# Normalizing the query features ahead of their transpose, in a fused linear-attention and MLP kernel

## The chip, the core and the metric

The kernel runs on one core of a Trainium2 chip. The metric is the device time of one execution in microseconds (us). PE is TensorE's matrix array (PEld its weight load), DVE is VectorE, ACT is ScalarE, POOL is GpSimd, SP is SyncE, which here only issues DMAs. PSUM is the memory that PE writes to, in eight banks.

## The reference, cut to what matters

```
x: 1 x 2048 x 448, bf16; H = 16 heads, Dh = 28
xn = layernorm(x)
q, k, v = split(xn @ wqkv)                       # per head 28 columns
phi(t) = [softmax(t @ w_phi), softmax(-t @ w_phi)]     # 2 x 28 features of a head
kv = phi(k)^T v ;  z = sum over tokens of phi(k)
o  = (phi(q) kv) / (phi(q) z + 1e-6)
out = x + o @ wo + mish(xn @ w1 + b1) @ w2       # w1: 448 x 1792, w2: 1792 x 448
```

## The kernel before, in words

The 2048 tokens make 16 tiles of 128 (t = 0 to 15), worked on in pairs (u = 0 to 7). All of x, the weights and the hidden activations `actT` (14 chunks x 2048 tokens) stay in SBUF. The work is cut into some 340 named steps, and a written-out list, `ORDER`, gives the order in which they are issued. Every engine then works through its own part of that order, strictly in sequence, and waits on semaphores where a step needs another's result. Nothing is scheduled at run time, so a step that waits holds everything behind it on its engine. DMAs of one queue are issued in the same manner: nearly all by SP.

The steps, by their names in `ORDER`:

- `lx..`, `lkm`, `lvm`, `lkt`, `lqT`, `l1..`, `l2`, `lo`: loads. The last letter is the queue (s for SP, a for ACT). `lqT0` to `lqT3` load the q weights transposed.
- `st`, `rs`, `xn`, `xt`: statistics of a pair (DVE, some tiles on ACT), reciprocal root (ACT or POOL), normalizing (DVE or POOL), and the transpose of the normalized pair (PE and an evacuation, or a DMA).
- `wtk`, `wmk`, `wmq`, `qd`, `bd`: w_phi is multiplied into the k and q weights once, giving `Wpk` and `Wpq`. This setup uses PE transposes (L556), passes L580 and evacuations L510/L512; `qd` (L286) doubles the last columns of the transposed q weights ahead of the q part.
- `k`, `v`, `q` with the parts A, B and H: projections of a pair. Each pass uses 64 rows of the array, two run at once (L423). The evacuation of k and q is the exponential on ACT, once with scale 1 and once with -1 (L618, L680).
- `kn`: one half (sign) of a pair's key exponentials is summed per head (DVE, L626), inverted (L628) and multiplied (POOL, L630).
- `kv`: phi(k)^T v of a pair, 32 small passes on 32-column strips of the array (L649). `kvz` copies the sum over all pairs out (L660) and turns it by a DMA into `KVZ` (L666).
- `e`: a DMA turns a tile's query exponentials (L688). There are three buffers for a pair's exponentials: `Eq0` and two rows of `actT`.
- `nd`: numerators and denominators of a query tile. 16 passes of 60 columns (L722) make, for each head and each sign, the numerator, the denominator and, by a column of ones, the sum of the query exponentials. Because two heads share a pass, half of `KVZ` is zero blocks. DVE then copies the sums, crosses them with the other sign's numerators, adds, inverts and scales (L738 to L749).
- `ot`, `wo`: the transpose of the output of a pair and its product with wo (L845, 64 rows).
- `f`: the MLP's first product, 64-row passes of 512 columns, with Mish and bias on ACT as evacuation (L699). `g`: its second product, 14 passes on all 128 rows into the same banks as `wo` (L828).
- `sto`, `stt`: stores, behind the last addition (L793).

## Time and profile before

| | us |
|---|---|
| median of 3 runs | 151.07 (150.71 to 151.2) |
| span of the profiled execution | 148.7 |
| PE busy | 144.0 |
| DVE busy | 102.7 |
| ACT busy | 74.7 |
| POOL busy | 38.9 |

The span runs from the first to the last instruction. The profiled execution's own device time is not recorded apart from its span; the median of the runs stands beside it, 2.4 us above. An engine's busy time is no measure of what it costs: what counts is which engine the chain of waits passes through. In the profile a line number is that of the kernel file, PS is PSUM, "SPq" is the issuing of a DMA by SP, and a transposed or plain load is done only when it has landed.

### The profile page before, as it was taken

The numbers are of one execution on the slowest core, as the hardware profiler recorded it, in microseconds if no ns is written. First come the engines' busy times: TensorE is split into PE (matmuls) and PEld (weight loads), VectorE is DVE, ScalarE is ACT, GpSimd is POOL, SyncE is SP. The second block draws the span as 40 slices with busy tenths as digits, with TensorE's granted clock in tenths as the row PEclk, the third lists the DMA queues.
The fourth block names the chain that finished last, engine by engine and source line by source line (L and its number), as shares of the span: only waits on it lengthen the run. The fifth ranks groups of instructions, "written<-read, shape, count | busy, mean of one in ns | idle before, by whom it ended". The sixth has DMA issues, their size and how long they took to land.

```text
span 148.7 us, 3864 instructions
## 1 busy us (share of the span) xinstructions
PE 144.0 (97%) x1669; PEld 74.2 (50%) x1669; DVE 102.7 (69%) x229; ACT 74.7 (50%) x91; POOL 38.9 (26%) x53
## 2 busy tenths in 40 slices
PE   6899999999999999999999999999999999999992
PEld 2365555555444555444444445545555555555561
DVE  0699898996999930407787989529983999930072
ACT  4997999779999999567747661002000000000000
POOL 4424465179999992000000000000000000000000
PEclk9999999999999999999999999999999999999999
DMA  4997997799699069499956053210013130551005
GB/s 131 245 278 216 119 185 149 126 170 344 103 188 196 14 52 132 85 239 295 195 98 125 4 62 62 43 23 0 7 37 86 35 93 0 123 127 58 4 10 175
DMA packets 39964, 17.23 MB, mean 116 GB/s; under 512 B 33932, under 2 KB 39180, under 8 KB 39948
## 3 DMA queue, kind: packets, MB, share of 16 engines
q1 hardware_dynamic: 39776, 16.89, 54.4%
q8 instruction: 13, 0.21, 0.6%
q10 hardware_dynamic: 172, 0.10, 0.2%
q14 instruction: 3, 0.02, 0.0%
HBM read 7.02 MB, written 1.84 MB: 60 GB/s over the span
## 4 chain that ended last, share of the span: by engine, by line
PE 92%; DMA 3%; DVE 2%; SPq 1%; issue 0%
PE PS L423 50%; PE PS L828 29%; PE PS L845 7%; DMA Wkv<-in_A_wqkv_dram 3%; PE PS L722 3%; PE PS L649 2%; PE PS L580 1%; DVE xn L497 1%; SPq L270 1%; PE PS L556 0%; PE PS L505 0%; DVE x_all L793 0%; DVE Eq L512 0%; DVE x_all L814 0%
## 5 line engine op out<-in xcount | busy, mean ns | idle before, releaser
L423 PE MATMUL PS<-xnT,W 64*128 64x512 bf16 x392 | 44.8, 377 | 0.0
L828 PE MATMUL PS<-W,actT 128*128 128x448 bf16 (+1 forms) x224 | 42.9, 351 | 0.0
L699 ACT ACTIVATE actT<-PS,b1T 128x1024 bf16<-128x1024 f32 x28 | 29.8, 1112 | 22.1 <-PE PS L423 22.1
L828 PEld LDWEIGHTS PS<-W,actT 128*128 128x128 bf16 x224 | 21.5, 98 | 19.8 <-issue 0.3
L423 PEld LDWEIGHTS PS<-xnT,W 64*128 64x128 bf16 x392 | 17.9, 94 | 21.9 <-PE PS L423 1.9
L630 POOL TENSOR_TENSOR actT<-actT,rSk 128x896 bf16<-128x896 bf16 x16 | 26.6, 1699 | 5.1 <-DVE rSk L628 5.1
L793 DVE TENSOR_TENSOR x_all<-PS,x_all 128x448 bf16<-128x448 f32 (+1 forms) x16 | 9.2, 613 | 15.2 <-PE PS L845 10.5
L626 DVE TENSOR_REDUCE Sk<-actT 128x32 f32<-128x896 bf16 x16 | 16.6, 1037 | 1.1 <-ACT actT L618 1.1
L618 ACT ACTIVATE actT<-PS 128x896 bf16<-128x896 f32 x16 | 13.7, 920 | 1.8 <-PE PS L423 1.7
L423 PE MATMUL PS<-Wpk,xnT 64*128 64x448 bf16 x112 | 13.2, 349 | 0.0
L423 PE MATMUL PS<-Wkv,xnT 64*128 64x448 bf16 x112 | 12.9, 349 | 0.0
L423 PE MATMUL PS<-Wpq,xnT 64*128 64x448 bf16 x112 | 12.6, 349 | 0.0
L738 DVE COPY Sq<-PS 128x16 f32<-128x16 f32 x32 | 4.0, 167 | 12.0 <-PE PS L722 12.0
L462 DVE BATCH_NORM_STATS2 stats<-x_all 128x6 f32<-128x448 bf16 x14 | 8.4, 601 | 3.4 <-DMA x_all<-in_A_x_dram 3.4
L746 DVE TENSOR_TENSOR v_all<-v_all 128x464 f32<-128x464 f32 x16 | 10.3, 641 | 0.6
L742 DVE TENSOR_TENSOR v_all<-PS,Sq 128x464 f32<-128x464 f32 x16 | 10.3, 641 | 0.5
L749 DVE TENSOR_TENSOR xn<-v_all,rden 128x448 bf16<-128x448 f32 x16 | 10.0, 625 | 0.6
L744 DVE TENSOR_TENSOR v_all<-PS,Sq 128x464 f32<-128x464 f32 x16 | 10.1, 629 | 0.0
L680 ACT ACTIVATE actT<-PS 128x896 bf16<-128x896 f32 x10 | 8.6, 930 | 0.1
L423 PEld LDWEIGHTS PS<-Wpq,xnT 64*128 64x128 bf16 x112 | 5.4, 94 | 5.0 <-ACT actT L680 0.2
L423 PEld LDWEIGHTS PS<-Wkv,xnT 64*128 64x128 bf16 x112 | 5.4, 94 | 5.1 <-ACT actT L618 0.2
L423 PEld LDWEIGHTS PS<-Wpk,xnT 64*128 64x128 bf16 x112 | 5.3, 94 | 5.1 <-issue 0.2
(83 smaller groups left out, 118.8 us busy)
## 6 DMA issues: line engine op xcount, KB each, us to landing
W<-in_B_w_dram SPq DMA_DIRECT2D x1, 1568.0 KB, 7.9
out_dram<-x_all SPq DMA_DIRECT2D x7, 224.0 KB, 2.2
W<-in_B_w_dram SPq DMA_DIRECT2D x1, 1344.0 KB, 7.0
x_all<-in_A_x_dram SPq DMA_DIRECT2D x4, 224.0 KB, 3.1
x_all<-in_A_x_dram SPq DMA_DIRECT2D x2, 448.0 KB, 4.9
Wkv<-in_A_wqkv_dram SPq DMA_DIRECT2D x2, 336.0 KB, 4.8
Wo<-in_A_wo_dram SPq DMA_DIRECT2D x2, 336.0 KB, 6.3
W<-in_B_w_dram SPq DMA_DIRECT2D x2, 224.0 KB, 4.1
```

The source lines that it names most:

```text
L423: ins = e.matmul(o, lhs(c, k), rhs(c, k), start=first and n == at[par][0], stop=last and n == at[par][-1])
L618: op("ACT", lambda e, s=s: e.activation(E_of(u)[:, s, :, :], two(b, D), ACT.Exp, scale=1.0 if s == 0 else -1.0), r=[pb(b), pb(b + 1)], w=[ ...
L626: op("DVE", lambda e: e.tensor_reduce(Sk[u][:, s, :], Eh(), AX.X, ALU.add), r=[("E", u, s)], w=[("Sk", u, s)], tag=f"Sk{u}.{s}")
L630: op("POOL", lambda e: e.tensor_tensor(Eh(), Eh(), ap_on(rSk[u][:, s, 0:1], [[1, 2 * H], [0, DH]]), ALU.mult), r=[("E", u, s), ("rSk", u, ...
L699: op("ACT", lambda e: e.activation(actT[:, fc, q * 1024:(q + 1) * 1024], bank(b, 2), ACT.Mish, bias=b1T[:, fc:fc + 1]), r=[("b1T",), pb(b) ...
L742: op("DVE", lambda e: e.tensor_tensor(tv(t1[i]), num(0), sx(1), ALU.mult), r=[pb(b), pb(b + 1), ("Sq", i, 1)], w=[("t1", i)], tag=f"ta{t}")
L744: op("DVE", lambda e: e.tensor_tensor(tv(t2), num(1), sx(0), ALU.mult), r=[pb(b), pb(b + 1), ("Sq", i, 0)], w=[("t2",)], tag=f"tb{t}")
L746: op("DVE", lambda e: e.tensor_tensor(t1[i], t1[i], t2, ALU.add), r=[("t1", i), ("t2",)], w=[("t1", i)], tag=f"tc{t}")
L749: op("DVE", lambda e: e.tensor_tensor(o_sb[(t // 2) % 2][:, t % 2, :].rearrange("p (h d) -> p h d", d=DH), t1[i][:, :, 0:DH], ap_on(rden[i ...
L793: op("DVE", lambda e: e.tensor_tensor(x_all[:, t, 0:n], bank(b)[:, 0:n], x_all[:, t, 0:n], ALU.add), r=[pb(b), ("x", t)], w=[("out", t)], ...
L828: ins = e.matmul(bank(b)[:, 0:width(t)], actT[:, fc, tok(t)], W2[:, fc, 0:width(t)], start=first and fc == 0, stop=last and fc == FC - 1)
L845: ins = e.matmul(bank(b)[:, 0:w], oT_of(u)[lo:hi, cc * P:(cc + 1) * P], Wo[lo:hi, cc, 0:w], start=first and n == at[par][0], stop=last and ...
```

## The change

- The query exponentials of a tile are now normalized ahead of the transpose (new step `qn`, one for each tile: sum and reciprocal on DVE, product on POOL, as for the keys). Both signs of a head lie side by side in 56 of 64 columns, so that a pass takes one head's whole feature row.
- `nd` keeps its 16 passes for a tile, but each has 30 columns. On DVE a reciprocal and one product are left. `KVT` and `KVZ` are half as large and have no zero blocks.
- `nd`'s results go to four buffers in place of two.
- `ORDER` is new throughout. Loads are the same, but x tiles 4 to 7 are issued by ACT and the others stand in another order; the statistics, normalizings and evacuations are dealt out otherwise (all v evacuations on ACT); `g` and `kv` are grouped otherwise.
- Options for other loads (`lkv`, `lfr`) and for a reciprocal root by single tiles are added, but no step of the list uses them; the bank choice is moved into a class with the same rules.

The core of the diff:

```
-NDW = 2 * (DH + 2)
+NDC = DH + 2
...
+    def q_norm(u, i):
+        n = u % 3
+
+        def Ei():
+            return Eq_of(u)[:, i, :, 0:QP].rearrange("p h (s f) -> p h s f", s=2)
+        op("DVE", lambda e: e.tensor_reduce(Sq[u][:, i, :].rearrange("p (h s) -> p h s", s=2), Ei(), AX.X, ALU.add),
+           r=[("Eq", n, i, s) for s in range(2)], w=[("Sq", u, i)], tag=f"Sq{u}.{i}")
+        op("DVE", lambda e: e.reciprocal(Sq[u][:, i, :], Sq[u][:, i, :]), r=[("Sq", u, i)], w=[("rSq", u, i)],
+           tag=f"rSq{u}.{i}")
+        op("POOL", lambda e: e.tensor_tensor(Ei(), Ei(), ap_on(Sq[u][:, i, 0:1], [[2, H], [1, 2], [0, DH]]), ALU.mult),
+           r=[("Eq", n, i, s) for s in range(2)] + [("rSq", u, i)], w=[("Eq", n, i, s) for s in range(2)], tag=f"phiq{u}.{i}")
...
-            for s in range(2):
-                for g in range(G):
-                    for r in range(2):
-                        at = (s * G + g) * NDW
-                        ins = e.matmul(bank(b + r)[:, at:at + NDW], EqT[64 * r:64 * r + QP, t, s * G + g, :],
-                                       ap_on(KVZ[64 * r:64 * r + QP, 2 * g + s, 64 * r:64 * r + 1], [[32, 2], [1, DH + 2]]),
-                                       start=True, stop=True)
+            for k in range(H // 2):
+                for r in range(2):
+                    at = 32 * (2 * r + k % 2)
+                    ins = e.matmul(bank(b + r)[:, k * NDC:(k + 1) * NDC], EqT[64 * r:64 * r + QP, t, k, :],
+                                   KVZ[64 * r:64 * r + QP, k // 2, at:at + NDC], start=True, stop=True)
...
-        for s in range(2):
-            op("DVE", lambda e, s=s: e.tensor_copy(
-                Sq[i][:, s, :].rearrange("p (r h) -> p r h", r=2),
...
+        op("DVE", lambda e: e.reciprocal(rden[:, t, :].rearrange("p (r k) -> p r k", r=2),
+                                         ap_on(bank(b)[:, DH:DH + 1], [[TCW, 2], [NDC, H // 2]])),
+           r=[pb(b), pb(b + 1)], w=[("rden", t)], tag=f"rd{t}")
+        op("DVE", lambda e: e.tensor_tensor(
+            o_sb[(t // 2) % NXN][:, t % 2, :].rearrange("p (r k d) -> p r k d", r=2, d=DH), num(0, DH),
+            ap_on(rden[:, t, 0:1], [[H // 2, 2], [1, H // 2], [0, DH]]), ALU.mult),
+           r=[pb(b), pb(b + 1), ("rden", t)], w=[("o", (t // 2) % NXN, t % 2)], tag=f"o{t}")
...
-pv table lx2s lba zero pm st2b lx3s lkms lps st3b lkts z12 pi b1 rs2p pw rs3a xn2d bd lx1s wtk0b lvms lx4s xn3d xt2b
+zero lx2a lx3a pp table lkms lps st2 lba pi st3b lkts rs3a pw lx1s rs2a lqT2 pm z12 bd xn3d pv lqT0 xn2p wtk0a lqT3
```

SP's queue at the start, before (x_all is x, Wkv the k and v weights, Wraw w_phi, WqT the transposed q weights):

```order
L270 DMA x_all<-in_A_x_dram 128x896 x2
L273 DMA Wkv<-in_A_wqkv_dram 128x3x448
L293 DMA Wraw<-in_A_w_phi_dram 112x4x28
L278 DMA Wkv<-in_A_wqkv_dram 64x896 x2
L270 DMA x_all<-in_A_x_dram 128x896
L273 DMA Wkv<-in_A_wqkv_dram 128x3x448
L270 DMA x_all<-in_A_x_dram 128x1792
L282 DMA_TRANSPOSE WqT<-in_A_wqkv_dram 128x448 x4
```

and after:

```order
L307 DMA Wkv<-in_A_wqkv_dram 128x3x448
L335 DMA Wraw<-in_A_w_phi_dram 112x4x28
L312 DMA Wkv<-in_A_wqkv_dram 64x896 x2
L304 DMA x_all<-in_A_x_dram 128x896
L324 DMA_TRANSPOSE WqT<-in_A_wqkv_dram 128x448 x4
L304 DMA x_all<-in_A_x_dram 128x1792 x2
L307 DMA Wkv<-in_A_wqkv_dram 128x3x448
```

The first two x loads have left the queue (ACT issues them), the k weights come first, and the four transposes stand ahead of the v weights and of the long x loads.

PE at the start, before (Wbd holds w_phi in blocks; the passes with WqT make the q weights, those with Eq0 the k weights):

```order
L580 MATMUL PS<-Wbd,Eq0 128x112 x8
L505 MATMUL PS<-ident,xn3 128x128 x7
L423 MATMUL PS<-Wkv,xnT 128x448 x2
L580 MATMUL PS<-Wbd,Eq0 128x112 x8
L423 MATMUL PS<-Wkv,xnT 128x448 x26
L423 MATMUL PS<-Wpk,xnT 128x448 x8
L580 MATMUL PS<-Wbd,WqT 128x112 x16
L423 MATMUL PS<-Wpk,xnT 128x448 x14
```

and after:

```order
L603 MATMUL PS<-Wbd,Eq0 128x112 x16
L528 MATMUL PS<-ident,xn3 128x128 x7
L528 MATMUL PS<-ident,xn2 128x128 x7
L603 MATMUL PS<-Wbd,WqT 128x112 x16
L435 MATMUL PS<-Wpk,xnT 128x448 x20
L435 MATMUL PS<-Wpq,xnT 128x448 x6
```

The v passes (Wkv) that filled PE between the setup's parts have moved behind the first k and q passes, and the q weights are made ahead of all of them.

POOL ahead of the key sums, before (rSk and a pair's number: a product of key exponentials):

```order
L473 TENSOR_TENSOR rstd<-lnv,mhalf 128x2
L630 TENSOR_TENSOR actT<-actT,rSk1 128x896
L630 TENSOR_TENSOR actT<-actT,rSk2 128x896 x2
L630 TENSOR_TENSOR actT<-actT,rSk0 128x896 x2
L630 TENSOR_TENSOR actT<-actT,rSk7 128x896
```

and after (Sq: a product of query exponentials):

```order
L718 TENSOR_TENSOR Eq0<-Eq0,Sq3 128x16x56 x2
L653 TENSOR_TENSOR actT<-actT,rSk2 128x896
L653 TENSOR_TENSOR actT<-actT,rSk3 128x896
L483 TENSOR_SCALAR lnv<-mv 128x2
L486 TENSOR_TENSOR rstd<-lnv,mhalf 128x2
L718 TENSOR_TENSOR actT<-actT,Sq2 128x16x56
L718 TENSOR_TENSOR actT<-actT,Sq1 128x16x56 x2
L718 TENSOR_TENSOR Eq0<-Eq0,Sq6 128x16x56
L653 TENSOR_TENSOR actT<-actT,rSk5 128x896
```

The products of queries stand between those of keys in one queue. In all, 8 query products stand among the 18 that come ahead of the first five `kv`.

## The prediction

> **What bounds the kernel now.** I read the page's busy line and its slices first, to see whether one engine fills the span.

> ```profile
> span 148.7 us, 3864 instructions
> PE 144.0 (97%) x1669; PEld 74.2 (50%) x1669; DVE 102.7 (69%) x229; ACT 74.7 (50%) x91; POOL 38.9 (26%) x53
> PE   6899999999999999999999999999999999999992
> PEclk9999999999999999999999999999999999999999
> ```

> PE does, at a full granted clock. Next comes the chain of waits, in order of time; its columns are start, length, and whose work it was.

> ```profile
> 10.42 3.32 PE PS L423 x34
> 13.75 0.89 PE PS L580 x16
> 14.64 36.25 PE PS L423 x370
> 50.89 0.88 PE PS L649 x96
> ...
> 67.30 3.93 PE PS L423 x36
> ...
> 88.60 1.89 PE PS L845 x20
> 90.49 0.22 PE PS L722 x16
> ...
> 102.94 10.70 PE PS L828 x56
> 113.64 0.33 PE PS L722 x16
> ...
> 142.98 2.42 PE PS L828 x14
> ...
> 145.42 0.56 DVE x_all L793
> ```

> From 10.42 to 145.4 us every piece is PE, one behind the other: nothing that DVE, ACT, POOL or a DMA does there ends last. So only four things can move the end: when this stream starts, how much PE work is in it, what PE loses between its instructions, and a new wait. The VectorE work that goes (seven steps an nd become two) is not on this list.

> The prices of PE work come from the same rows. A 448-column pass takes 1.89/20 = 0.0945 us, a 512-column pass 3.93/36 = 0.109, a kv pass (L649) 0.88/96 = 0.0092. An nd (L722, 16 passes of 60 columns, two at a time) takes 0.22. But right behind an L828 group it takes 0.33, against 0.22 elsewhere: going between passes on all 128 rows (L828) and passes on 64 rows costs about 0.1 us.

> **Term 1, the start of the stream.** Before, the stream starts when the setup (transposed weights, the k projection's two halves) allows v and k; the q weights' 16 passes (L580) stand inside it at 13.75. After, they stand ahead of it, and the first stream pass is a k pass, behind these 16. What the 16 wait for is the copy L286 (now L328), which needs all four transposed loads of WqT. The timeline of the head, and the page's DMA part with the time from issue to landing at the end of a row:

> ```profile
> 0.80 0.87 SPq L270 DMA_DIRECT2D x_all<-in_A_x_dram  x2
> 1.72 0.43 SPq L273 DMA_DIRECT2D Wkv<-in_A_wqkv_dram  x1
> 2.19 0.49 SPq L293 DMA_DIRECT2D Wraw<-in_A_w_phi_dram  x1
> 2.72 1.19 SPq L278 DMA_DIRECT2D Wkv<-in_A_wqkv_dram  x2
> 3.95 0.59 SPq L270 DMA_DIRECT2D x_all<-in_A_x_dram  x1
> ...
> 5.59 5.11 SPq L282 DMA_TRANSPOSE WqT<-in_A_wqkv_dram  x4
> ...
> 13.13 0.23 DVE L286 COPY WqT<-WqT 128x256 bf16<-128x256 bf16 x1
> 13.68 0.96 PE L580 MATMUL PS<-Wbd,WqT 112*128 112x112 bf16 x16
> ...
> Wkv<-xn SPq DMA_TRANSPOSE x4, 3.0
> ...
> KVZ<-KVT SPq DMA_TRANSPOSE x1, 3.2
> ```

> After, SP issues Wk, Wraw, two tails and one x load ahead of them; two x loads move to ACT's queue, Wv and the long x loads move behind. By the spacing of these rows: 0.80 + 0.47 (Wk) + 0.53 (Wraw) + 1.23 (tails) + 0.6 (x) = 3.6 for the first transpose, 5.11 x 3/4 = 3.8 more for the fourth, near 7.5; it lands 3.0 later (the 3.0 and 3.2 of transposes that nothing delays), 10.5. From the copy's start to the first pass is 13.68 - 13.13 = 0.55, the 16 passes 0.89: the stream starts at 11.95. The second thing it needs, the k weights' halves, hangs on x tile 7 (timeline again):

> ```profile
> 5.03 0.56 ACT L453 ACTIVATE junk<-x_all 128x448 bf16<-128x448 bf16 x1
> ...
> 6.75 0.29 ACT L476 ACTIVATE lnv<-mv,eps_col 128x2 f32<-128x2 f32 x1
> ...
> 7.07 0.20 ACT L478 ACTIVATE rstd<-lnv 128x2 f32<-128x2 f32 x1
> ...
> 8.54 0.60 ACT L510 ACTIVATE Eq<-PS 112x512 bf16<-112x512 bf16 x1
> ...
> 9.59 0.61 DVE L512 CAST Wpk<-PS 128x448 bf16<-128x448 f32 x1
> ...
> 18.45 1.73 POOL L492 TENSOR_SCALAR xn<-x_all,rstd,shift 128x448 bf16<-128x448 bf16 x3 [0.38 <-DVE shift L485]
> ```

> On ACT the statistics take 7.27 - 5.03 = 2.24, a second pair's Ln and Exp 0.5, and two 1024-column evacuations (0.60 for 512, so about 1.0 each) 2.0. On DVE the second half of Wpk stands behind a shift that waits for POOL, which first normalizes a pair (1.73) and takes a reciprocal root (0.7 and a sum of 0.2): 2.24 + 0.9 (three normalizing steps) + 0.3 + 1.73 + 1.0 + 0.2 + 0.65 = 7.0 from x's landing. If x3 lands by 4.9 this is covered by the WqT path. ACT's first statistics could start at 5.03 without waiting, so x3 was there by then; now it shares the engines with Wk on SP's queue, and is not sure to be. I take 11.95 and a range of 11.2 (all loads 0.7 quicker) to 13.0.

> Against the 10.42 of before: +1.53, two v passes that ran ahead of it move behind the start, 2 x 0.0945 = +0.19, and the 16 q-weight passes leave the stream, -0.89, with the 3.32 - 34 x 0.0945 = 0.11 that PE lost ahead of them. Net +0.72.

> **Term 2, switches of shape.** Before, the stream has five groups of L828 (42, 56, 28, 84, 14 passes; nine changes, as the last ends the stream) and three of kv (six changes). After, three groups of L850 (98, 84, 42; five changes) and two of kv (160 and 96; four): six fewer, at 0.1 us: -0.6. For the kv changes I take the same price; no row isolates it, its ends are 0 and 0.2, so this term lies between -0.4 and -1.0.

> **Term 3, the nd passes.** Their columns halve, 60 to 30, their number (16 per tile, two at once) stays. By columns a pair falls from 0.22/8 = 0.0275 to about 0.0148 us (0.0945 x 2/448 = 0.00042 per column): 16 x 8 x 0.0127 = -1.6. At the other end it stays, 0, if a pair's weight load or hand-over sets the pace: each pass loads 128 columns of weights, as before. The row itself, 0.0275, is the shortest spacing on one part of the array that the trace shows (kv, four at once: 4 x 0.0092 = 0.037). I take -0.2, near the end that a row shows. [...] No row here has fewer than 56 moving columns on a tile of the stream, so the trace doesn't decide it.

> **Term 4, what could be waited for.** Each query tile gets a sum, a reciprocal and a product, as each key half has now (groups of instructions first: busy time, mean ns of one, idle time before; then two rows of the timeline):

> ```profile
> L699 ACT ACTIVATE actT<-PS,b1T 128x1024 bf16<-128x1024 f32 x28 | 29.8, 1112 | 22.1 <-PE PS L423 22.1
> L630 POOL TENSOR_TENSOR actT<-actT,rSk 128x896 bf16<-128x896 bf16 x16 | 26.6, 1699 | 5.1 <-DVE rSk L628 5.1
> ...
> L626 DVE TENSOR_REDUCE Sk<-actT 128x32 f32<-128x896 bf16 x16 | 16.6, 1037 | 1.1 <-ACT actT L618 1.1
> ...
> L462 DVE BATCH_NORM_STATS2 stats<-x_all 128x6 f32<-128x448 bf16 x14 | 8.4, 601 | 3.4 <-DMA x_all<-in_A_x_dram 3.4
> ...
> L628 DVE RECIPROCAL rSk<-Sk 128x32 f32<-128x32 f32 x16 | 5.7, 353 | 0.6
> ...
> L473 POOL TENSOR_TENSOR rstd<-lnv,mhalf 128x2 f32<-128x2 f32 x6 | 4.2, 706 | 0.5
> ...
> L699 ACT ACT_TABLE_LOAD x2 | 2.6, 1283 | 0.0
> ...
> 59.26 1.84 DVE L660 TENSOR_SCALAR KVT<-PS,epsT 30x224 bf16<-30x224 f32 x4 [5.97 <-PE PS L649]
> ...
> 61.13 1.23 SPq L666 DMA_TRANSPOSE KVZ<-KVT  x1
> ```

> POOL gets 16 products of 1.7 = 27 us more, and does one every 26.6/16 = 1.66 us; DVE needs 1.04 + 0.35: POOL sets the pace of both kinds. In the new order 18 products (8 of them of queries) stand ahead of the first five kv, 24 ahead of the last three. My count: DVE is through with Wpk's half and an evacuation 0.7 behind the stream's start, at 12.6; eight statistics at 0.6 with an aggregate of about 0.13 beyond it, and 1.0 of small steps, take it to 19.5; a pair normalized on POOL, 1.73, and the first product begins at about 21.3; four products to 27.9, a reciprocal root 0.9, fourteen products: 52.0. PE meets the first kv behind 322 passes of 448 and 84 of 512 columns: 11.95 + 30.4 + 9.2 = 51.6, and the fourth, which needs the 18th product, 0.9 later, 52.5. Six products more end at 61.9; PE has 82 passes of 512 (8.9) ahead of its next kv, 62.0, and the last one at 62.6. The first nd: kv's end 62.9, plus 5.1 for the copies and the transpose (from L660's start at 59.26 to the landing at 61.13 + 3.2), = 68.0; PE is there at 68.7. Covers of 0.4 to 0.6 us everywhere: no wait, but no room. If POOL were 5% slower, kv would wait 1 us. I take +0.1.

> Hidden, each with its cover: three v evacuations go from DVE to ACT and two more table loads (1.28 each) come, under the 22.1 us that ACT waits for PE; the DVE steps of nd that go lay under PE in any case; W2 and Wo, issued ahead of the last query turns, land long before L850. If ACT had no such idle, the table loads would cost 2.6.

> **Sum.** +0.72 - 0.6 - 0.2 + 0.1 = 0.0. The profiled execution's span is 148.7; around it lie 151.07 - 148.7 = 2.4 us up to the median, start and end being as before: 151.1 us. I call 0.3% (0.45 us) the least that can be told from no change.

> **Rivals.**
> 1. nd halves with its columns. For it: PE is column-bound in every other row (a pair of 448 takes 0.189, a pair of 512 0.218). Against: no spacing that short is seen. 151.1 - 1.4 = 149.7. Chance 0.26.
> 2. Slower: the head is late, because Wk, x2 and x3 now share the DMA engines and x3 lands near 6. ACT's statistics, then POOL's two steps, then DVE's half of Wpk follow in line. It decides from an x3 landing of 4.9 on; at 6.0 the stream starts at 13.0: 152.2. For it: DVE's copy L328 and its shift stand in line ahead of Wpk's half, so any late load holds it. Against: x3 was early before. Chance 0.16.
> 3. Slower: POOL's products run late and the first five kv wait, some 0.9 us: 152.0. For: covers of 0.5. Against: POOL's pitch was steady at 1.66 beside a busy DVE. Chance 0.10.
> 4. Faster: the head's loads, no longer behind the two x loads on SP, land 0.7 earlier: stream at 11.2, 150.35. Chance 0.13.

> The forecast itself, 151.1, is the likeliest with 0.35. **How the numbers follow.** Same: the forecast, less its edges, with some of the rivals' near edges, 0.35. Faster: rivals 1 and 4, 0.39. Slower: rivals 2 and 3 and a few hundredths of other waits, 0.26. The forecast's own range, from the bounds of terms 1 and 2, is 150.3 to 152.0. To hold 8 in 10 it must reach into rival 1, to 149.5, and to rival 2's 152.2.

> **What would show it.** The first k pass at 11.95, with the copy L328 ending just ahead (term 1); 0.1 us lost at five and four changes only (term 2); an nd at 0.20 to 0.22 in the chain, or 0.12 if rival 1 holds (term 3); PE with no wait on POOL's products ahead of kv, on KVZ ahead of nd, or on ACT (term 4). A PE idle of more than 0.5 us after the start, or an nd of 0.12, makes the forecast wrong.

## The result, and the profile after

The changed kernel takes 160.53 us (160.03 to 162.23) where the kernel before takes 151.12 beside it: the ratio is 1.0648, with a 95% interval of 1.0585 to 1.0711. It is 9.4 us slower; the forecast was 151.1, with 149.5 to 152.2 as its range. The ratios here and below leave out executions more than 1.5% above the fastest of their kernel (one in experiment 1, two in experiment 7, its profiled one among them); the medians take them in.

The profiled execution is the longest of its four, 162.23 us with a span of 160.3. The shortest, 160.03, has a span of 158.1. PE's mean clock was 0.968 in the one and 0.989 in the other (0.968 and 0.978 in the two between them), and 1.000 in the profile before. The page's busy line and its slices:

```profile
span 160.3 us, 3831 instructions
PE 148.1 (92%) x1669; PEld 77.7 (49%) x1669; DVE 88.1 (55%) x170; ACT 79.2 (49%) x94; POOL 69.9 (44%) x77
...
PE   7749999997699996999989999999999999999993
...
PEclk9996999999789998799999999999999999999999
```

PE has dips at three places (slices 2 and 3, 10 and 11, 16), and right behind each the granted clock is down. A table by stretches (length, busy time and count of PE, PEld, DVE, ACT, POOL, then the clock, DMA share and GB/s) shows the three windows:

```profile
11.37:14.78 3.41, 3.41 (x34) 2.68 (x33) 2.62 (x8) 2.82 (x6) 2.82 (x6) 0.52 0.80 305
42.09:45.50 3.41, 3.41 (x24) 1.71 (x20) 3.34 (x6) 0.94 (x2) 3.41 (x3) 0.52 1.17 142
62.57:65.98 3.41, 3.41 (x20) 1.25 (x18) 3.34 (x6) 1.16 (x2) 3.41 (x3) 0.52 0.35 98
```

PE's waits, where the kernel before had 1.4 and 0.4 us in all:

```profile
PE PS L435 <- DMA xnT<-xn: 2.7, 1, 2.7
PE PS L603 <- ACT Eq L533: 2.2, 2, 1.9
PE PS L672 <- issue: 1.9, 1, 1.9
...
PE PS L435 <- ACT actT L702: 0.7, 1, 0.7
```

**The head.** The chain of waits (start, length, whose work) ahead of the stream:

```profile
1.27 4.81 DMA x_all<-in_A_x_dram
...
6.10 0.68 ACT junk L466 x2
...
8.15 0.21 ACT rstd L493
...
9.54 1.74 POOL xn L510 x3
...
11.56 0.73 POOL rstd L486
...
12.31 0.16 DVE shift L502
12.47 0.54 DVE Wpk L535
13.01 0.53 DVE xnT L535
```

The first k pass starts at 13.78, behind the last of these, DVE's copy of the turned x tiles. The chain does not come from the WqT loads (they landed at 10.15), but from the x tiles on ACT's queue, which landed at 6.08.

**The pairs that DVE normalizes among POOL's products.** The timeline of DVE, POOL and SP's queue there:

```profile
26.36 3.39 POOL L653 TENSOR_TENSOR actT<-actT,rSk 128x896 bf16<-128x896 bf16 x2
...
26.88 3.20 DVE L520 TENSOR_SCALAR xn<-x_all,mv,rstd 128x448 bf16<-128x448 bf16 x3
...
31.65 0.23 POOL L483 TENSOR_SCALAR lnv<-mv 128x2 f32<-128x2 f32 x1 [1.89 <-DVE mv L477]
...
35.50 2.86 DVE L520 TENSOR_SCALAR xn<-x_all,mv,rstd 128x448 bf16<-128x448 bf16 x3
...
38.39 1.23 SPq L540 DMA_TRANSPOSE xnT<-xn  x1
...
39.82 1.70 POOL L718 TENSOR_TENSOR Eq<-Eq,Sq 128x896 bf16<-128x896 bf16 x1 [1.78 <-DVE Sq L716]
```

Three steps that took 0.86 to 0.90 us in most places of the kernel before take 3.20 and 2.86. Each consists of three pieces; the first two end 0.03 to 0.13 behind the end of a product (at 28.20 and 29.79 behind 28.07 and 29.75, at 36.48 and 38.07 behind 36.35 and 38.04), the third runs when POOL has stopped. Behind the triples POOL stands idle for 1.89 and 1.78 us, since DVE's sums come late, and the pair of x tiles 0 and 1 is turned only from 38.39 on: PE waits 2.7 us for it. The chain of waits runs through both triples into the first pass behind that pair, `k0B`:

```profile
26.96 3.12 DVE xn L520 x3
...
35.50 2.86 DVE xn L520 x3
...
38.39 3.05 DMA xnT<-xn
```

**The five kv.** The timeline of PE:

```profile
58.48 1.27 PE L672 MATMUL PS<-actT,v_all 128*30 128x56 bf16 x119
61.63 0.48 PE L672 MATMUL PS<-actT,v_all 128*30 128x56 bf16 x41 [1.88 <-issue]
```

PE stops in the middle of a kv, after 119 of 160 passes, at a pass that carries no wait, while no semaphore is outstanding ("issue").

**The nd passes** in the chain, away from 128-row groups: 0.19 for 16 passes, where 0.22 stood.

```profile
88.74 0.19 PE PS L756 x16
```

### The profile page after: what moved, and what is told of

Read it like the earlier page. It is cut to its first block, busy times and chain, and to the rows that moved or that the text cites. A ratio compares the mean times of both kernels' runs of the same rounds, so it can differ in the third digit from the quotient of the medians.

```text
span 160.3 us, 3831 instructions
## 1 busy us (share of the span) xinstructions
PE 148.1 (92%) x1669; PEld 77.7 (49%) x1669; DVE 88.1 (55%) x170; ACT 79.2 (49%) x94; POOL 69.9 (44%) x77
## 3 DMA queue, kind: packets, MB, share of 16 engines
HBM read 7.02 MB, written 1.84 MB: 55 GB/s over the span
## 4 chain that ended last, share of the span: by engine, by line
PE 61%; DVE 17%; DMA 10%; ACT 6%; issue 3%; POOL 2%; ACTq 0%; DVEq 0%; POOLq 0%
PE PS L850 26%; PE PS L435 24%; PE PS L867 7%; DVE xn L520 4%; DVE Sq L714 4%; DMA x_all<-in_A_x_dram 3%; DMA Wkv<-xn 3%; DMA EqT<-actT 3%; ACT actT L641 2%; DVE stats L475 2%; DMA xnT<-xn 2%; PE PS L672 2%; PE PS L756 2%; DVE Sk L649 1%; DVE KVT L683 1%
## 5 line engine op out<-in xcount | busy, mean ns | idle before, releaser
L435 PE MATMUL PS<-xnT,W 64*128 64x512 bf16 x392 | 46.9, 386 | 0.7 <-ACT actT L702 0.7
L850 PE MATMUL PS<-W,actT 128*128 128x448 bf16 (+1 forms) x224 | 42.5, 351 | 0.0
L850 PEld LDWEIGHTS PS<-W,actT 128*128 128x128 bf16 x224 | 21.7, 98 | 20.2 <-issue 0.6
L435 PEld LDWEIGHTS PS<-xnT,W 64*128 64x128 bf16 x392 | 19.5, 96 | 22.1 <-issue 2.2
L653 POOL TENSOR_TENSOR actT<-actT,rSk 128x896 bf16<-128x896 bf16 x16 | 26.7, 1710 | 0.0
L718 POOL TENSOR_TENSOR actT<-actT,Sq 128x896 bf16<-128x896 bf16 x10 | 16.8, 1708 | 7.2 <-DVE Sq L716 7.2
L649 DVE TENSOR_REDUCE Sk<-actT 128x32 f32<-128x896 bf16 x16 | 16.5, 1031 | 0.0
L641 ACT ACTIVATE actT<-PS 128x896 bf16<-128x896 f32 x16 | 13.8, 943 | 5.3 <-PE PS L435 3.8
L435 PE MATMUL PS<-Wkv,xnT 64*128 64x448 bf16 x112 | 14.0, 365 | 0.0
L435 PE MATMUL PS<-Wpq,xnT 64*128 64x448 bf16 x112 | 13.9, 353 | 0.0
L714 DVE TENSOR_REDUCE Sq<-actT 128x32 f32<-128x896 bf16 x10 | 10.4, 1036 | 2.4 <-ACT actT L702 2.4
L718 POOL TENSOR_TENSOR Eq<-Eq,Sq 128x896 bf16<-128x896 bf16 x6 | 10.2, 1703 | 3.1 <-DVE Sq L716 3.1
L763 DVE RECIPROCAL rden<-PS 128x16 f32<-128x16 f32 x16 | 4.1, 255 | 13.3 <-PE PS L756 13.3
L766 DVE TENSOR_TENSOR xn<-PS,rden 128x448 bf16<-128x448 f32 x16 | 10.0, 624 | 1.5 <-DMA Wkv<-xn 0.9
L520 DVE TENSOR_SCALAR xn<-x_all,mv,rstd 128x448 bf16<-128x448 bf16 (+2 forms) x11 | 7.9, 768 | 1.4 <-ACT rstd L493 1.4
```

The costliest lines, as they stand in the source:

```text
L435: ins = e.matmul(o, lhs(c, k), rhs(c, k), start=first and n == at[par][0], stop=last and n == at[par][-1])
L520: op("DVE", lambda e, t=t, lo=lo, hi=hi, at=at: e.tensor_scalar(X[:, at:at + hi - lo], x_all[:, t, lo:hi], mv[:, t, 0:1], rstd[:, t:t + 1] ...
L641: op("ACT", lambda e, s=s: e.activation(E_of(u)[:, s, :, :], two(b, D), ACT.Exp, scale=1.0 if s == 0 else -1.0), r=[pb(b), pb(b + 1)], w=[ ...
L649: op("DVE", lambda e: e.tensor_reduce(Sk[u][:, s, :], Eh(), AX.X, ALU.add), r=[("E", u, s)], w=[("Sk", u, s)], tag=f"Sk{u}.{s}")
L653: op("POOL", lambda e: e.tensor_tensor(Eh(), Eh(), ap_on(rSk[u][:, s, 0:1], [[1, 2 * H], [0, DH]]), ALU.mult), r=[("E", u, s), ("rSk", u, ...
L714: op("DVE", lambda e: e.tensor_reduce(Sq[u][:, i, :].rearrange("p (h s) -> p h s", s=2), Ei(), AX.X, ALU.add), r=[("Eq", n, i, s) for s in ...
```

## The experiments

### 1. The held steps moved to ScalarE

```
-... kn3.0 v4Aa xn7d ... k5A xn0d ...        # DVE
+... kn3.0 v4Aa xn7a ... k5A xn0a ...        # ACT: shift and all six pieces
```

> The changed kernel, but the two pairs that VectorE normalizes among POOL's products (x tiles 14, 15 and 0, 1; 3.20 and 2.86 us there, 0.9 elsewhere) are normalized on ScalarE, shift included, at the same places of the order. Theory A (each of VectorE's normalizing instructions there is held until the POOL product that runs beside it ends; this makes POOL starve after it, the turned tiles and the key products late, and TensorE idle twice, and each idle of over 2 us halves the clock for 3.4 us): the 2.7 us wait ahead of k0 and the 2.2 us wait ahead of kv3 shrink below 1 us or go, the clock is halved at most once (at the head), the gaps of POOL after 29.8 and 38.0 (1.9 and 1.8 us) go: 152.5 to 155. Theory B (the head is the cause, everything later only follows it): 159.5 to 161, the two waits stay. Theory C (POOL's doubled number of products is too much for it): the wait ahead of kv3 stays or grows, 157 to 160.

Measured: 160.73 us, ratio 1.0627 (1.056 to 1.0695). No gain. The wait for the turned pair went (2.7 to 0.2), POOL ran with no gap over 0.4 us from 22.8 to 72 us, and the clock was 1.00 in the profiled execution, all as theory A has it; yet PE got as many waits at other places:

```profile
PE PS L678 <- issue: 2.2, 1, 2.2
...
PE PS L435 <- ACT v_all L539: 1.7, 1, 1.7
PE PS L435 <- ACT actT L647: 1.6, 1, 1.6
```

ACT evacuates every k, q and v bank in this stretch, and in the changed kernel it is full already: in the table by stretches its column (the fifth number) has 17.95 of 18 us.

```profile
20.00:38.00 18.00, 18.00 (x192) 8.98 (x190) 16.92 (x27) 17.95 (x24) 15.13 (x14) 1.00 0.72 164
```

What it gets besides delays its evacuations, for which PE then waits. The stop in the kv stayed, with POOL no longer late. As a test of theory A the edit was poor: it took one load off and put another on.

### 2. The head's loads alone

```
-zero lx2a lx3a pp table lkms lps ...
+zero pp table lx3s lx2s lkms lps ...
```

> The changed kernel, but the two first x loads stand at the front of SyncE's queue, ahead of Wk, as in the kernel before, in place of ScalarE's queue. Theory B: x tiles 6, 7 land near 4 instead of 6.1, the first k pass starts near 12.5 instead of 13.8, the clock is not halved at the head, and the later waits shrink with it: 154 to 157. Theory A: only the head's own part comes back, 1.0 to 2.0 us: 158.5 to 159.5, with the waits ahead of k0 and kv3 and two halvings of the clock still there. If the transposed loads of WqT, now 0.9 us later on the queue, set the start: first k pass at 12.5 to 13, gain under 1.

Measured: 160.18 us, ratio 1.0593 (1.0531 to 1.0654). The first k pass came at 12.60, 1.2 earlier, and the clock was not halved at the head; but x tiles 0 and 1 were still turned late, k0B still started at 41.51 (41.57 before the edit), and the time moved by 0.4, less than the interval tells from nothing. Theory B falls: the head is late, but the stream behind it waits at 41.5 for something that does not depend on it.

### 3. Idle stretches filled with passes over zeros

```
+ ... wtk1a z8 ...  z12 k0B ...  z8 kv3 ...     # 8, 12 and 8 passes of 512 columns
```

> The changed kernel with three idle stretches of TensorE filled with passes over zeros: 8 (1.7 us at full clock) in the wait after the second transpose of Wk, 12 ahead of k0B, 8 ahead of kv3. No data moves earlier. Theory D (of the 11.6 us lost, some 4 to 5 are the clock, halved for 3.4 us after each idle stretch: 0.55 and 0.75 at the head, 1.7 and 1.7 later): the clock stays at 1.0 or is halved at the start alone, the waits stay as long (filled): 155.5 to 157. If the clock is not what costs (the halved windows fall where TensorE would wait anyway): 159.5 to 161. If the filling passes themselves come in the way: above 161.

Measured: 158.96 us, ratio 1.0529 (1.0462 to 1.0595), the clock 1.000 in every execution. It is 1.6 us below the changed kernel, and the spread went: 158.7 to 159.3 here, 160.0 to 162.2 without. The expected 4 to 5 us were read off the one execution that had three halved windows; the others have one to three by their mean clocks. As a price of the clock the 1.6 is a net. In the kv the filling passes brought a wait of their own, for a PSUM bank that ACT had not yet emptied, and with their own time 3.2 us stand there in place of the stop of 1.9:

```profile
56.67 1.21 PE L672 MATMUL PS<-actT,v_all 128*30 128x56 bf16 x128
59.47 1.69 PE L404 MATMUL PS<-zeros 128*128 128x512 bf16 x7 [1.59 <-ACT actT L702]
```

The traces show the price of one halved window inside the stream: from the fifth kv to the sixth, 82 passes of 512 columns, there pass 10.8 us in the changed kernel, where one stands, and 9.1 here, 1.7 less. The first line shows something else: the first four kv, 128 passes, ran without the stop behind the 119th. The 20 filling passes ahead of them (8 and 12) had moved PE's code on by 40 instructions, which experiment 9 takes up.

### 4. The disputed step by itself

In the kernel before, one instruction of 448 columns was put between the sum and the reciprocal of each key product, in three forms in turn, and three of each again behind the last product.

```
+ x: tensor_scalar(jj0, x_all[4], mean, rstd, subtract, mult)
+ r: tensor_scalar(jj1, x_all[4], mean, None, subtract, add, accum_out=jacc)
+ t: tensor_tensor(junk0, x_all[4], x_all[5], add)
```

> The kernel before, with one VectorE instruction of 448 columns put between the reduce and the reciprocal of each of the 16 key products, so that it runs beside the POOL product ahead; three forms in turn: the normalizing form (one tensor, two scalars), the same tensor and size with a sum written out beside it, and a sum of two tensors in SBUF; and three of each again after the last key product, where POOL has nothing to do. Theory A: the normalizing form takes 0.25 alone, and beside a POOL product about what is left of that (0.3 to 1.7, ending when the product ends); the form with the sum takes the same (0.5 to 0.6) in both places. [...] If a busy VectorE or memory in general were the cause: all three forms grow by the same share.

Groups of DVE's instructions from 30 to 62 us, while POOL works (busy time, mean ns of one, idle before), and then from 62 to 71, when it does not:

```profile
L629 DVE TENSOR_SCALAR jj<-x_all,mv,rstd 128x448 bf16<-128x448 bf16 x7 | 7.3, 1042 | 0.0
L636 DVE TENSOR_TENSOR junk<-x_all 128x448 bf16<-128x448 bf16 x4 | 4.6, 1156 | 0.0
L632 DVE TENSOR_SCALAR_CACHE_REDUCE jj<-x_all,mv 128x448 bf16<-128x448 bf16 x4 | 2.6, 660 | 0.0
...
L632 DVE TENSOR_SCALAR_CACHE_REDUCE jj<-x_all,mv 128x448 bf16<-128x448 bf16 x3 | 2.0, 673 | 0.0
L629 DVE TENSOR_SCALAR jj<-x_all,mv,rstd 128x448 bf16<-128x448 bf16 x3 | 1.2, 393 | 0.0
L636 DVE TENSOR_TENSOR junk<-x_all 128x448 bf16<-128x448 bf16 x3 | 1.2, 387 | 0.0
```

The first two forms take 0.39 alone (0.25 had been expected for the first) and 1.04 or 1.16 beside a product; the form with a sum takes 0.67 and 0.66. The timeline shows what sets the 1.04: the instruction starts at 37.75 and ends at 38.79, the product beside it ends at 36.96 + 1.70 = 38.66.

```profile
36.96 1.70 POOL L652 TENSOR_TENSOR actT<-actT,rSk 128x896 bf16<-128x896 bf16 x1 [0.59 <-DVE rSk L650]
37.75 1.04 DVE L629 TENSOR_SCALAR jj<-x_all,mv,rstd 128x448 bf16<-128x448 bf16 x1
```

All seven of the first form end 0.13 behind the product, all four of the second 0.25 behind it. Here each starts 0.8 us into its product; in the changed kernel the pieces start 0.1 to 0.9 into theirs and end 0.03 to 0.13 behind them as well. So what sets the end is not a slower DVE but the end of POOL's instruction, for which two of the forms wait; the third, 0.66 beside a product and 0.67 alone, does not. What makes them wait no trace here shows.

### 5. The unheld form in the changed kernel

```
-  tensor_scalar(xn, x, mean, rstd, subtract, mult)
+  tensor_scalar(xn, x, rstd, None, mult, add, accum_out=jacc)      # pairs 0 and 7 only
```

> The changed kernel, but VectorE normalizes the two pairs that stand among POOL's products with the form that also writes out a sum, at the same places. This form has one operation on the elements, so x times the reciprocal root is computed for these four tiles and the subtraction of the mean is left out. From the probe (0.67 alone and beside a product, where the other form took 0.39 alone and 1.04 beside one): three pieces and three sums read out make about 1.7 us a pair where 3.2 and 2.9 were. Theory A (the held form makes x tiles 0 and 1 late): POOL's gaps of 1.9 and 1.8 shrink to under 0.7, the wait ahead of k0B goes from 2.7 to under 1, the stall at the five kv stays at about 2: 157.5 to 159.3. If ScalarE's load is what binds this stretch in any case (the run with normalizing on ScalarE got other waits of 1.75 and 1.9 instead): 159.5 to 160.5, and a new wait for an exponential or a copy of ScalarE appears ahead of k or q.

Measured: 156.38 us, ratio 1.0364 (1.0296 to 1.0432): 4.2 us less than the changed kernel, more than the 1.2 to 3.0 expected. The kernel leaves out the mean of these four tiles. The wait for the turned pair is gone from PE's list, and POOL has no gap over 0.35 us from its first product, at 24.0, to 75.4. Theory A holds: the same place, the same engine, the same columns, with a form that is longer by itself (0.67 against 0.39), and 4.2 us come back, with what follows from it: in the profiled execution the clock was 1.0 from 15.8 on, and the stop in the kv was 1.2 long in place of 1.9.

### 6. The five kv set apart

```
-kv5 kn0.0 kv2 kv4 kv1 kn6.0 kn7.1 kv3 f1.7A f0.3B ...
+kv5 kn0.0 kv2 f1.7A kv4 kv1 f0.3B kn6.0 kn7.1 kv3 ...
```

> The changed kernel, with the first five kv not in one run of 160 passes: after two of them stand 6 FFN passes, after two more another 6, then the fifth. In all traces of the changed order so far TensorE stops after 119 of these 160 passes for 1.9 to 2.2 us with nothing to wait for (no semaphore at that pass), and starts again 2.5 us after a 16 KB packet began on the queue of instructions. Theory E (TensorE runs out of code: 160 passes are 320 instructions in 1.4 us, and a 16 KB piece holds 256 of 64 bytes and takes 2.5 us): each gap there under 1.0 and in all at least 1 us less: 158.0 to 159.5, and fewer halvings of the clock. Theory C (kv waits for POOL's products): the stop stays, split over the places, 160 to 161.

Measured: 160.67 us, ratio 1.0616 (1.0553 to 1.068). The run cannot tell: f1.7's Mish writes over the row of `actT` from which kv1 reads its key exponentials, and ahead of kv1 it changes what kv1 computes and makes PE wait 2.7 us for ACT at that place.

### 7. No query products on POOL

```
-        op("POOL", lambda e: e.tensor_tensor(Ei(), Ei(), <reciprocals>, ALU.mult), ...)    # in q_norm
```

> The changed kernel without POOL's 16 products of the query tiles (the sum and the reciprocal stay; the normalization of the numerators is left out), all else in the same order: POOL has 27 us less to do and VectorE's normalizing runs beside fewer products. If POOL's load, through its own pace or through what it holds up on VectorE, is the largest part: 153.5 to 156, no wait ahead of k0B. If head, code loading and ScalarE make up most of it: 157.5 to 159.5, with the stop at the five kv still there.

Measured: ratio 1.043 (1.0332 to 1.0528), a median of 158.93; its executions at 156.75 (clock 1.00) to 159.78 (0.978). The wait ahead of k0B is gone, as it is without held steps. But with 27 us less on POOL the stop in the kv is still there, at the same pass:

```profile
54.78 1.14 PE L672 MATMUL PS<-actT,v_all 128*30 128x56 bf16 x119
58.54 0.59 PE L672 MATMUL PS<-actT,v_all 128*30 128x56 bf16 x41 [2.62 <-issue]
```

Theory C falls for this stop: kv does not wait for POOL's products.

### 8. Six kv in one run, in the kernel before

```
-... kv5 kn7.1 kv0 kv2 ... kv7 kv4 kv6 ...
+... kn7.1 ... kv5 kv0 kv2 kv7 kv4 kv6 ...
```

> The kernel before, with its first three kv moved behind to join the next three, so that six stand in one run of 192 passes (384 instructions); their products are done long before by then. Theory E: a stop of 1 to 2.5 us inside the run, without a semaphore, ending about 2.5 us after an instruction packet of 16 KB: 152 to 154, perhaps a halved clock behind it. Without it: no stop, two changes of tile shape fewer, 150.5 to 151.

Measured: 151.35 us, ratio 1.0013 (0.9988 to 1.0039): no stop, against what theory E expected in this plain form. That the run is long is not enough. Counting PE's recorded instructions (two for a pass, and the separate waits of its sequencer), in the changed order the stop comes behind number 1216, whatever the time and the neighbours: at 59.56, 58.75, 59.48, 56.27 and 55.73 us in the changed kernel and in experiments 1, 2, 5 and 7. There the 256 instructions from 960 to 1216 took 2.0 to 2.2 us. Here the two pieces that the run falls into, counted from the same numbers, took 4.9 and 3.6 us. That led to experiment 9.

### 9. PE's code shifted by 56 instructions

```
+ ... wtk1a tiny ...          # 28 passes of 2 columns over zeros in PE's idle time at the head
```

> The changed kernel with 28 passes of 2 columns over zeros in TensorE's wait after the second transpose of Wk (1.9 us idle there). They move no other work, but every later instruction of TensorE stands 56 places further on in its code. In the five traces of the changed order that share TensorE's list, the stop in the five kv comes at the same place of the list, 1216 recorded instructions from its start, whatever the time (55.7 to 59.6 us) and whatever POOL has to do; the piece of 256 ahead of it took 2.0 to 2.2 us. Moved by 56, the piece holds 72 instructions of FFN and query passes (about 3.9 us) ahead of its kv, 4.7 us in all, and the next one 137 of kv and 119 of FFN passes. Theory E (code comes in pieces of 256 instructions, and one that is run in less than about 4 us ends in a wait for the next; the run of six kv in the kernel before did not stop because its pieces took 4.9 and 3.6 us): no stop in the five kv, 158.0 to 159.2. If the stop belongs to kv1 or kv3 themselves (their data, their bank): it stays at 2, 160 to 161.

Measured: 157.02 us, ratio 1.0388 (1.0369 to 1.0407), 3.5 us less than the changed kernel; more than the 1.3 to 2.5 expected. In the profiled execution the halved window behind the stop went with it, and PE's wait for ACT behind KVZ fell from 0.7 to 0.2. PE's timeline:

```profile
57.85 1.60 PE L682 MATMUL PS<-actT,v_all 128*30 128x56 bf16 x160
```

All 160 passes run without a stop. No step of the kv, of POOL or of the data was moved; what changed is where the pieces of code begin. (The 28 passes also take a PSUM bank. Behind the head that only renames the banks of all steps, by one fixed exchange; which steps share a bank stays as it was.) Three more things speak for code and not for a bank. In the six profiled runs that stop behind number 1216 (the five, and experiment 11) PE starts again 2.2 to 2.6 us after a 16 KB packet began on the queue of instructions, whether the stop lasts 1.2 or 2.6 us. In the changed kernel that queue moved 13 such packets, while PE went from the 174th to the 3241st of its 3366 recorded instructions: on the mean one for 256 (by these counts, some 64 bytes for each). And in experiment 3, with the code moved by 40, the piece that ends behind number 1216 took 4.0 us, and PE did not stop there. Theory E holds in these runs: PE ran out of code. How much code PE holds at a time no run here shows.

### 10. Three edits in one

The edits of 2, 5 and 9 together.

> The changed kernel with the three edits in one: the two first x loads at the front of SyncE's queue, the normalizing beside products in the form that writes out a sum (the mean left out for these four tiles), and the 28 small passes that shift TensorE's code. If the three causes add up (1.2 for the head, 4.2 for the held form, 1.2 to 2 for the code, and a clock halved once less, 0.5 to 1): 152.5 to 154.5, with the wait ahead of k0B and the stop at kv gone and 0.5 to 1 us left of waits for ScalarE ahead of nd3 and f1.13. If another bound stands behind them (ScalarE, or POOL's 24 products ahead of the last kv, that end near 64): 154.5 to 156.5, with a new wait of over 1 us.

Measured: 153.31 us, ratio 1.0148 (1.0123 to 1.0174). The three bring back 7.2 of the 9.4 us; singly they gave 0.4, 4.2 and 3.5, 8.1 in all. The mean of four tiles is left out here too. What is left of PE's waits:

```profile
PE PS L596 <- DMA Wkv<-in_A_wqkv_dram: 1.9, 1, 1.9
PE PS L445 <- DMA xnT<-xn: 1.0, 1, 1.0
```

The first is the head, in the longest of its executions (153.98; the others 153.25 to 153.33).

### 11. Eight columns in an nd pass

```
-  matmul(bank(b + r)[:, k * NDC:(k + 1) * NDC], EqT[...], KVZ[..., at:at + NDC])
+  matmul(bank(b + r)[:, k * NDC + 22:(k + 1) * NDC], EqT[...], KVZ[..., at + 22:at + NDC])
```

> The changed kernel with 8 in place of 30 moving columns in each pass of nd (22 columns of each head's numerators are left out). If a least time of a pair of passes holds (0.19 us for 16 passes, 24 ns a pair, now that 30 columns stand where 60 took 0.22): nd stays at 0.19 in the chain. If columns count (the 30 columns at 0.42 ns each are 12.6 ns, far below 24): nd falls to 0.13 or less. Time as the changed kernel, 160 to 162, in both cases within what its clock varies.

Measured: 163.11 us in one execution at a clock of 0.958; 22 of the 30 columns are left out. The chain of waits:

```profile
89.79 0.18 PE PS L756 x16
```

0.22 with 60 columns, 0.19 with 30, 0.18 with 8: a pair takes 24 ns at 30 columns and 23 at 8, so columns no longer count there.

### 12 to 15. The rest: an unheld form that computes everything, and the old head

```
12: + ACT copies rstd of pairs 0 and 7 into a column of a PSUM bank
    - tensor_scalar(xn, x, mean, rstd, subtract, mult)
    + scalar_tensor_tensor(xn, x, mean, <PSUM column, repeated>, subtract, mult)
    + f0.3B f0.9A f0.3A f0.3H ahead of kv5
13: 12, and ORDER up to wmq1a as in the kernel before
14: 12, and ORDER up to the sixth pass of k2A as in the kernel before
15: 14, with the form of experiment 5 in place of the PSUM column
```

> The changed kernel, with all of the computation, in which the two pairs beside products are normalized by VectorE with the reciprocal root read from a PSUM column (one operand in SBUF, one in PSUM; ScalarE copies the two roots there first), and 20 FFN passes (f0.3, and f0.9 but for its last two) moved ahead of the five kv, so that these straddle a piece of TensorE's code. If the hold is of the form with one tensor in SBUF on both sides, this one runs at about 0.5 to 0.7 for 448 columns beside a product, as the form with the sum did: no wait ahead of k0B, no stop in the kv, 154 to 156. If an instruction with two tensors is held whatever memory the second lies in: 157 to 159, with the pieces again at 1.0 to 1.7. A bank of PSUM is kept for about 3 us; if TensorE wants it by then, a wait of up to 2 us.

> The same, with the steps up to the q weights' passes in the order of the kernel before (x loads first, v passes of two pairs ahead of the k weights, q weights inside the stream), the rest in the changed order. If the 2 us that the three edits together left (153.3 against 151.3) are the head's: the first stream pass stands near 9.6 to 10.5 again, TensorE idles under 0.5 after it, 151.0 to 153.0. If POOL's products, which start no earlier, bind the kv and nd behind them: 153 to 155, with a wait ahead of kv or nd.

> As the run before, with the order of the kernel before kept seven steps longer (through the second k pair's 6 passes). It tells whether the seam between the two orders costs: within 0.5 of the run before if not; a wait for ScalarE or VectorE at the seam would go or come with it, 1 us either way.

> As the run before (old order through the second k pair, FFN passes ahead of the five kv), but the two pairs beside products use the form that writes out a sum (mean left out for these four tiles), so ScalarE copies no roots and no PSUM bank is kept. In the two runs with the old head the stream started at 9.6 to 10.0, 4 us earlier than in the changed order, and lost it again between 21 and 41 us, in waits for ScalarE's copies of v (1.5 to 2.4 us), with k0B at 39.4 to 40.7 as in every run of the changed order. If these waits came from ScalarE's extra copies and the kept bank: k0B near 37.5 and 151.5 to 153. If the new order's load on ScalarE, VectorE and POOL binds that stretch whenever the stream starts: k0B at 39 to 40 still, 153 to 155.5.

Measured: 156.58 (1.0366; 1.0331 to 1.0402), 156.63 (1.0365; 1.032 to 1.041), 155.81 (1.0336; 1.0282 to 1.039) and 154.29 us (1.0198; 1.0169 to 1.0227). In 12 the three pieces take 1.40 us beside products where 3.20 stood, after DVE has waited for ACT's copy:

```profile
26.12 3.35 POOL L663 TENSOR_TENSOR actT<-actT,rSk 128x896 bf16<-128x896 bf16 x2
28.16 1.40 DVE L525 SCALAR_TENSOR_TENSOR xn<-x_all,mv,PS 128x448 bf16<-128x448 bf16 x3 [1.47 <-ACT PS L501]
```

So this form, with its second operand in PSUM, is not held: the first piece is over at 28.84, the product beside it at 29.48. And the kv run without a stop behind the FFN passes moved ahead of them. (In 15 PE's records show a gap of 0.3 us behind number 1216, in a piece that took 4.2.) With the old head the first stream pass stands at 9.6 to 10.1 where run 12 has it at 14.06 (some 1.4 us of setup passes then lie inside the stream). But k0B comes at 40.65, 39.37 and 38.72, after 40.74 in run 12: most of the earlier start is lost again, in 13 and 14 in waits for ACT's v evacuations (2.4 and 1.5 us), in 15 for a query exponential (1.2). Taking the PSUM copy (and with it the mean of four tiles) away from 14 brought about 1.5. None of these orders beats the kernel before. So the last 2 us are not explained in full. The head has a part (experiment 10), and the stretch from 21 to 41 us, where ACT, DVE and POOL are all nearly full (17.95, 16.92 and 15.13 of the 18 us from 20 to 38 in the changed kernel), takes back most of an earlier start; how the rest splits was not settled.

### 16. The loads of W2 and Wo moved

In the changed kernel, about the time that PE waits for its code, the DMA engines look like this (58.9 to 60.3 us: packets, MB, share of the 16 engines):

```profile
q1 hardware_dynamic: 549, 0.49, 103.3%
q8 instruction: 1, 0.02, 4.9%
```

```
- ... e4 ... e5 ... l2s ... los ... e8
+ ... l2s los e3 e2 e12 e13 e4 e5 ... e8
```

> The changed kernel with the loads of W2 and Wo issued on SyncE three turned query tiles earlier (near 42 us instead of 52 to 59), so that they land near 52. In the changed order they fill the DMA engines from about 55 to 65 us, and the 16 KB packet of TensorE's code begins 1.7 us after TensorE has entered the piece ahead; in the run without query products, where these loads landed by 56.1, the packet began at 56.0. Theory F (the code waits behind the data on the DMA engines): the packet begins within 0.5 us, and the stop falls from 2 to under 1: 158.3 to 159.7. Theory E alone (a piece run in 2.1 us always stops, since the code takes 3.5 to 4 us by itself): the stop stays at 1.3 to 2.1: 159.7 to 160.7. If the turned query tiles come late behind the loads (queued on SyncE): a new wait for a query buffer on ScalarE or PE, 161 or more.

Measured: 166.52 us, ratio 1.1015 (1.097 to 1.106). The third case came, at a far higher price than expected: six turned query tiles stood behind these loads and landed at 51.5 to 57.7, the buffers of the query exponentials came free late, and PE waited 7.9 us in one piece. In the kv itself there was no stop any more:

```profile
PE PS L435 <- ACT actT L702: 7.9, 1, 7.9
...
66.84 1.48 PE L672 MATMUL PS<-actT,v_all 128*30 128x56 bf16 x160
```

The piece of 256 was again run in 2.04 us, but its successor's packet had begun 1.2 us before PE entered it, where it began 1.2 to 2.4 us after in the five runs that stopped. A packet behind bulk loads thus fits all these times (in experiment 7 it began at 56.04, when the last of Wo landed at 56.08; in the kernel before, one began at 70.31, 4.7 us after its piece, when W2 landed at 70.35, and did no harm, as that piece took 9.4). It is not isolated: PE's 7.9 us of waiting stand ahead of this piece too.

## Why the prediction was wrong

**Term 4, the waits, is the step that failed**: +0.1 us was put down for all of them. Two prices were missing from it. The first is DVE's. The count gave DVE 1.04 + 0.35 for each product, let POOL set the pace, and asked of POOL only whether it keeps its 1.66. The two pairs that DVE normalizes among products have no price of their own there; the only one that the sum has for such a triple is the 0.9 of term 1. POOL did keep its pace (26.7 us for 16 products). But a triple among products takes 2.9 to 3.2 (experiment 4 gives the price of a piece: 0.39 alone, 1.04 beside a product that had 0.9 left), the sums behind it come late, and POOL, the turned tiles and PE wait in turn. Worth 4.2 us (experiment 5). The 18th product ended at 58.08 in place of the 52.0 counted, and that this lateness cost the kv nothing was luck: PE came to them at 58.48 in place of 51.6. The profile before had a hint. In its head one triple of these steps stands beside another work of POOL, and takes 1.25 where the others take 0.86 to 0.90; its first piece ends at 8.51, POOL's instruction at 8.38:

```profile
7.06 1.31 POOL L539 TENSOR_TENSOR Wbd<-Wraw,mask 112x224 bf16<-112x224 bf16 x2 [0.36 <-DMA Wraw<-in_A_w_phi_dram]
7.75 1.25 DVE L497 TENSOR_SCALAR xn<-x_all,mv,rstd 128x448 bf16<-128x448 bf16 x3
```

**Rival 3** (kv waits for POOL's products, 152.0) expected a wait at the right place for the wrong reason. PE did stand in the five kv, for 1.9 us, but for its own code. That is the second missing price: no term of the sum held the supply of instructions, and a row of five kv was counted at its passes alone. Worth 3.5 us with what follows from it (experiment 9).

**A cover of term 4 was read at the wrong place.** The three v evacuations and two table loads that go to ACT were put under the 22.1 us that ACT waits for PE. In the profile before all of that stands with the Mish, from 43 us on; from 20 to 38 us, where the new work lands, ACT was busy for 16.19 of 18 us. What this cost by itself was not measured; experiments 13 and 14 have waits of 2.4 and 1.5 us for these evacuations.

**Term 1, the head**: 11.95 was forecast, 13.78 measured. WqT's landing (10.5; measured 10.15) was right and did not matter. The assumption that failed is that x lands by 4.9: it landed at 6.08, and the chain was the one that rival 2 describes, step by step. Rival 2 put the start at 13.0, where DVE's half of Wpk does end. The other 0.8 is a step that it left out, DVE's copy of the turned x tiles (0.53, to 13.54), and the hand-over; the q weights' 16 passes, at half clock, run up to the same time. But the price was mis-sized the other way: set right alone, the head gives 0.4 us, which may be nothing, and not 1.2 (experiment 2), as k0B waits for its tiles at 41.5 either way. The forecast took each microsecond of a later start as one of a later end, which holds only while PE is what ends last.

**Term 2, the switches**, was right: each change between 128-row groups and others costs 0.09 to 0.12 by the start times of the groups, at four of the five places of L850; the fifth stands behind an nd and can't be told apart. The kv changes, for which no row was at hand, cost 0.09 going in and 0.12 coming out, so the price taken for them holds.

**Term 3, the nd passes**: 0.19 for 16 passes, a gain of 16 x 0.03 = 0.5 us where 0.2 was taken. Rival 1 (0.12 a tile) is wrong: a pair of passes took 28 ns at 60 columns, 24 at 30 and 23 at 8 (experiment 11), so that at 30 the columns set the pace no longer.

**What was not in the forecast at all** is the clock. It was 1.0 throughout before, and I took it as given. In the profiled execution PE's waits of 2.7 and 1.9 us inside the stream were each followed by 3.41 us at half clock, and one such window cost it 1.7 us more (experiment 3). Its share of the median was not isolated (experiment 3 gives a net of 1.6).

**The range.** From the bounds that terms 1 and 2 state, it comes to 149.95 to 152.35 and not to 150.3 to 152.0; 160.53 lies far outside both, by waits that no bound held.

## What to carry to other kernels

A step that is moved has to be priced at its new place: look at which instructions of the other engine will run beside it, and whether its form (one tensor from SBUF to SBUF, two tensors in SBUF, a sum written out, an operand in PSUM) is one that waits for POOL: here the first two ended 0.13 and 0.25 us behind POOL's product (experiment 4), and the last two did not wait (experiments 4 and 12). In a run of very short passes count instructions as well as columns: here 256 of them (128 passes with their weight loads) in 2.0 to 2.2 us were followed by a stop of 1.2 to 2.6 us, while 256 in 3.6 us or more cost at most 0.3. Bulk loads on the DMA engines may have made it worse; that was not isolated. And where several engines are full in a stretch, an earlier start of the stream is worth little; the row to look at is the first pass behind that stretch.
